# Block 0 of a state-space scan feeding a feed-forward product: the second scan moved into the second product, an idle product dropped, weight loads sent behind VectorE's steps

## The chip, the cores and the metric

The kernel runs on one core of a Trainium2 chip. Its time is device time in microseconds (us), given as the median of several runs of the whole program. One further execution was profiled: its trace says when each instruction of TensorE (PE, with its weight loads as PEld), VectorE (DVE), ScalarE (ACT), GpSimd (POOL) and the DMA queue of SyncE (SP) started, how long it took, and what ended the idle time before it. Each engine executes its own instructions strictly in the order in which the program holds them, and waits there for what the others must have done.

## The reference

The first half is a Mamba-2 scan over 4 batches, 8 heads, 768 tokens, with 32 values and 16 states per head, in chunks of tokens:

```python
cum = np.cumsum(log_a_chunk, axis=-1)
L = np.exp(cum[..., :, None] - cum[..., None, :]) * causal
M = einsum('bhin,bhjn->bhij', C, B) * L
y = einsum('bhij,bhjd->bhid', M, x) + einsum('bhin,bhnd->bhid', C, state) * np.exp(cum)[..., None]
state = np.exp(sum(log_a_chunk)) * state + sum_j(B_j x_j * np.exp(cum_end - cum_j))
```

The heads of one token are then laid side by side (256 values per token, 3072 tokens), and the second half is a feed-forward layer with 2048 inner columns:

```python
h = x @ w_in                                  # 256 -> 2048
g = h * np.clip(h + 3, 0, 6) / 6              # hardswish
out = g @ w_out                               # 2048 -> 256
```

The inputs of the scan are 32-bit floats. Both weight matrices arrive as 64-bit floats, and the kernel turns them into 32-bit ones itself.

## The kernel before

**Blocks.** The 768 tokens of a batch are cut into six blocks of 128. Block k holds these 128 tokens of all four batches, 512 rows of the feed-forward layer. Within a block the scan works in two halves of 64 tokens. While the feed-forward layer of block k runs, the scan of block k+1 is done between its products.

**Row sums.** The logarithms of `a` lie with one row per batch and head (32 rows, 768 columns, `a_sb`). VectorE's scan (`add_up`, L282) multiplies a running sum by `run` (one, and zero at each start of 64) and adds the logarithm. It is done in two parts: the first 256 columns (blocks 0 and 1), then the other 512 (blocks 2 to 5). The results of the second part go to DRAM by `store_rows` (L299, L301), and come back spread over partitions by `load_decay` (L314, the tile `L` of a block) and `load_eto` (L321, the tile `eto`); `rows(c)` calls both. They are also turned by TensorE (`turn_cum`, L329, into the bank `f1`) and copied with their sign changed by VectorE (`by_token`, L332, into `cum_n`). Blocks 0 and 1 get their exponents of decays from products of TensorE (`diff_*`), which ScalarE takes through the exponential (`diff_exp`, L393).

**A block's scan.** `scores(c)` (L558) makes the products of B and C, and L576 those of B and x for the new state. `multiply(c)` (L607) multiplies the four score banks with the decays on VectorE. `mix(c)` (L653) multiplies the result with x, and `from_state` (L531) adds what comes from the state; for that `csT` is C times the decay since the start (`fade`, L509). `keep(c)` (L667) copies the results on ScalarE into `yT`. `renew(c)` (L628, L586) makes the next state, which `carry` (L431) and `ends` (L424) on GpSimd use later. `conceal` (L158) masks a decay tile on GpSimd, `decay` (L413) exponentiates it on ScalarE.

**Weights.** `load_w(i)` (L139) loads an eighth of the weights, 1 MB, into one of three buffers `raw`: 0 to 3 are quarters of `w_in`, 4 to 7 of `w_out`. `decode(i)` turns it into 32-bit floats in steps, each up to a `yield`: a copy of the top halves on ScalarE (L198), masks on VectorE (L215, L217, L201, L205), two activations on ScalarE (L221, L223), and two last steps on VectorE (L228, L236). `weights(i, n)` does the next n steps.

**Feed-forward, block 0.** The first product (`mlp_in`, L677) makes 16 stripes f of 128 inner columns by 512 rows in plain 32-bit arithmetic, in the four banks f0 to f3 in turn; each stripe is two passes, for the two halves of the 256 inputs. ScalarE's ramp (L784) and VectorE's product with it (L789) make `gT`. The second product (`first_out`, L802) follows in four parts i (a quarter of `w_out` each) for four batches b. Between these calls stand the steps of the last weights and the scan of block 1. From block 1 on both factors of the first product are split into three parts (`in_parts`, L714 on ScalarE, L717 and L720 on VectorE, for the weights; `split_y`, L734, L735, L737, for the rows), and each stripe has three pairs of products (L745) in one of six banks: `squares` makes the first two pairs, `cross` the third after `enlarge` (L762 on VectorE for the first two stripes of block 1, L765 on ScalarE otherwise). So stripe f+6 of block 1 needs the bank of stripe f, which is free after its L789. The second product of these blocks works on sums of quarters (`weight_sums`, L828; `g_sums`, L848 on GpSimd; `wide_units`, L993).

**Order.** The order on each engine is that of the calls, written out by hand; only the waits are derived, from which instruction writes and reads which tile. Tiles with the same tag share a place. SyncE issues nearly all DMAs from one queue, in the order of the calls; a DMA at its head that has to wait for its buffer, or for data, holds all that stand behind it.

The tile `pre`, in which `a_sb`, `run` and the sums lie, shares its place with `gT` of block 0. `busy(n, bank)` (L521) runs n products of the identity with itself, whose results nobody reads.

```python
    multiply(0)
    load_w(3)
    c_ps = ps.tile([P, NC, G], FP32, name="c_ps", tag="f1")
    turn_cum(c_ps)
    busy(1, ps.tile([P, NB * P], FP32, name="d", tag="f0"))
    by_token(c_ps)
    weights(0, 1)
    weights(1, 1)
    mix(0)
    keep(0)
```

## Time and profile before

| | before |
|---|---|
| median of 3 runs | 337.82 us |
| the three runs | 338.59, 337.82, 337.63 us |
| the profiled execution's own time | 337.39 us |
| its span in the trace | 335.6 us |
| TensorE busy | 329.2 us (98%) |
| VectorE busy | 264.3 us (79%) |
| ScalarE busy | 208.0 us (62%) |
| GpSimd busy | 133.4 us (40%) |
| block 0's scores start (L558) | 15.07 us |
| block 0's own products start (L653) | 19.15 us |
| block 0's first product, start and length (L677) | 22.06 us, 27.74 us |
| block 0's second product starts (L802) | 49.80 us |
| block 1's first product starts (L745) | 82.68 us |

The times in the lower rows are counted from the start of the span. The span is a little shorter than the time of the execution, which also holds what lies before the first and after the last instruction. Busy time is a sum over the whole span, and says which engine could be the bound; which wait ends last in one place is read from the chain of work that ended last (each piece was released by the one before it) and from the instructions in order of time. In those, the number in brackets is the idle time of the engine before the instruction, with what ended it.

### The profile page before, as it was taken

How to read it: one execution, taken by the hardware profiler on the slowest of the kernel's cores; microseconds unless marked ns; L12 is line 12 of the kernel's file. 1: busy time of each engine (PE TensorE's matmuls, PEld its weight loads, DVE VectorE, ACT ScalarE, POOL GpSimd, SP SyncE). 2: the span in 40 equal slices, each digit the busy share in tenths (PEclk: the TensorE clock that was granted, in tenths of full speed). 3: DMA queues.
4: the chain of work that ended last, by engine and by line, in shares of the span. 5: the costliest groups of instructions: out<-in, count | busy, mean ns of one | idle time of the engine just before them, and what ended most of it. 6: DMA issues, size and time to landing. Idle time of an engine off the chain costs nothing.

```text
span 335.6 us, 8324 instructions
## 1 busy us (share of the span) xinstructions
PE 329.2 (98%) x3361; PEld 272.0 (81%) x3361; DVE 264.3 (79%) x416; ACT 208.0 (62%) x447; POOL 133.4 (40%) x125
## 2 busy tenths in 40 slices
PE   7999999999999999999999999999999999999995
PEld 5454788888888888888888888888888888899995
DVE  6999999998499739769949558938678958599974
ACT  4778878657986671677662477643487221677661
POOL 2400000290284799079983078771058740000000
PEclk9999999999999999999999999999999999999999
DMA  8998977042590216249107258100142001210001
GB/s 175 169 320 187 188 261 177 2 56 75 144 139 1 58 40 133 34 70 81 35 2 164 35 77 76 32 4 10 28 71 19 2 4 17 29 20 0 2 0 63
DMA packets 89605, 25.15 MB, mean 75 GB/s; under 512 B 82208, under 2 KB 85952, under 8 KB 89056
## 3 DMA queue, kind: packets, MB, share of 16 engines
q1 hardware_dynamic: 85184, 23.33, 37.4%
q10 hardware_dynamic: 4384, 1.31, 1.8%
q8 instruction: 26, 0.43, 0.5%
q14 instruction: 11, 0.09, 0.1%
HBM read 21.33 MB, written 3.29 MB: 73 GB/s over the span
## 4 chain that ended last, share of the span: by engine, by line
PE 96%; DVE 2%; issue 1%; POOL 0%; ACT 0%; POOLq 0%
PE h L745 33%; PE wc L993 8%; PE o L802 8%; PE wb L993 8%; PE h L677 8%; PE wa L993 8%; PE o_end L957 6%; PE wb L1001 3%; PE y L653 3%; PE y L531 2%; PE cb L558 2%; PE d L356 1%; DVE q_part L885 1%; PE d L521 1%; PE y L576 1%; PE d L369 1%
## 5 line engine op out<-in xcount | busy, mean ns | idle before, releaser
L789 DVE SCALAR_TENSOR_TENSOR gT<-gT,h 128x512 f32<-128x512 f32 x96 | 64.9, 684 | 24.9 <-ACT gT L784 23.3
L784 ACT ACTIVATE gT<-h,half 128x512 f32<-128x512 f32 x96 | 65.5, 684 | 23.4 <-PE h L745 21.3
L765 ACT ACTIVATE h<-h 128x512 f32<-128x512 f32 x66 | 38.3, 585 | 36.9 <-PE h L745 36.7
L745 PE MATMUL h<-y_hi,w_part 128*128 128x512 f32 x160 | 51.0, 404 | 0.0
L745 PE MATMUL h<-y_less,w_part 128*128 128x512 f32 x160 | 50.1, 400 | 0.0
L745 PE MATMUL h<-y_lo,w_part 128*128 128x512 f32 x160 | 49.5, 395 | 0.0
L848 POOL TENSOR_TENSOR s<-gT 128x512 f32<-128x512 f32 x16 | 24.9, 1559 | 48.0 <-DVE gT L789 48.0
L745 PEld LDWEIGHTS h<-y_lo,w_part 128*128 128x128 f32 x160 | 30.0, 188 | 6.9
L745 PEld LDWEIGHTS h<-y_hi,w_part 128*128 128x128 f32 x160 | 30.0, 188 | 6.8 <-DVE gT L789 0.2
L745 PEld LDWEIGHTS h<-y_less,w_part 128*128 128x128 f32 x160 | 29.1, 188 | 6.1 <-DVE h L762 0.3
L413 ACT ACTIVATE L<-L,cum_n 128x64 f32<-128x64 f32 x128 | 31.7, 337 | 0.0
L802 PE MATMUL o<-w_out,gT 128*128 128x256 f32 x128 | 28.8, 381 | 0.0
L677 PE MATMUL h<-yT,w_in 128*128 128x256 f32 (+1 forms) x94 | 27.8, 457 | 0.0
L802 PEld LDWEIGHTS o<-w_out,gT 128*128 128x128 f32 x128 | 24.1, 190 | 3.4
L677 PEld LDWEIGHTS h<-yT,w_in 128*128 128x128 f32 x94 | 17.8, 190 | 9.7 <-issue 6.9
L431 POOL TENSOR_TENSOR tmp<-state,eto 128x256 f32<-128x256 f32 x5 | 3.2, 632 | 56.2 <-ACT eto L417 48.7
L848 POOL TENSOR_TENSOR gT<-gT 128x512 f32<-128x512 f32 x16 | 23.9, 1501 | 0.7
L158 POOL TENSOR_SCALAR_AFFINE_SELECT L<-L 64x1024 f32<-64x1024 f32 (+1 forms) x16 | 20.6, 1297 | 8.2 <-DMA L<-cum_d 7.7
L885 DVE TENSOR_TENSOR q_part<-gT,q_part 128x256 fp32r<-128x256 f32 x24 | 21.6, 928 | 0.0
L424 POOL TENSOR_TENSOR bs<-B,L 128x128 f32<-128x128 f32 x24 | 12.7, 549 | 21.8 <-ACT L L413 14.1
L957 PE MATMUL o_end<-v_pair,g_pair 128*128 128x256 f32 x120 | 21.1, 281 | 0.0
L848 POOL TENSOR_TENSOR s<-s,gT 128x512 f32<-128x512 f32 x16 | 20.6, 1292 | 0.0
(164 smaller groups left out, 636.7 us busy)
## 6 DMA issues: line engine op xcount, KB each, us to landing
raw<-in_moe_w_out_dram SPq DMA_DIRECT2D x4, 1024.0 KB
L<-cum_d SPq DMA_DIRECT2D x8, 512.0 KB
xt<-in_x_dram SPq DMA_DIRECT2D x6, 512.0 KB
raw<-in_moe_w_in_dram SPq DMA_DIRECT2D x3, 1024.0 KB
out_dram<-back SPq DMA_DIRECT2D x128, 16.0 KB
pairs<-in_C_dram SPq DMA_DIRECT2D x40, 32.0 KB
eto<-cum_e SPq DMA_DIRECT2D x20, 64.0 KB
B<-in_B_dram SPq DMA_DIRECT2D x5, 256.0 KB
```

What stands on the lines that cost most here:

```text
L158: nc.gpsimd.affine_select(out=t[rows], in_=t[rows], pattern=pattern, compare_op=ALU.is_ge, fill=-1e5, base=base, channel_multiplier=-1)
L413: nc.scalar.activation(Ls[c][:, b, h], Ls[c][:, b, h], AF.Exp, bias=cum_n[:, c, g:g + 1])
L677: nc.tensor.matmul(out=h[:, t:t + n], lhsT=w_in[f // FP][:, j, f % FP * P:(f % FP + 1) * P], rhs=yTs[k][:, j].rearrange("p b i -> p (b i)" ...
L745: nc.tensor.matmul(out=hs_[k, f], lhsT=w[j][:, f % FP * P:(f % FP + 1) * P], rhs=y[:, j], start=(start and j == 0), stop=True, skip_group_ ...
L765: nc.scalar.activation(h, h, AF.Copy, scale=1.0 / EPS + 1.0)
L784: nc.scalar.activation(gTs[k][:, f], h, AF.Relu, bias=half, scale=1.0 / 6.0)
L789: nc.vector.scalar_tensor_tensor(out=g, in0=g, scalar=1.0, in1=h, op0=ALU.min, op1=ALU.mult)
L802: nc.tensor.matmul(out=o[:, b % 2], lhsT=gTs[0][:, f, b * P:(b + 1) * P], rhs=w_out[:, f], start=(f == 0 and b % 2 == 0), stop=True, skip_ ...
L848: nc.gpsimd.tensor_tensor(out=o, in0=p_, in1=q_, op=op)
L885: nc.vector.tensor_tensor(out=l[:, j], in0=g[:, j], in1=h[:, j].bitcast(FP32), op=ALU.subtract)
L957: nc.tensor.matmul(out=ends_["cross" if n == 2 else "squares"][b], lhsT=g_parts[t][n][:, b * P:(b + 1) * P], rhs=w, start=(t == 0 and b < ...
L993: nc.tensor.matmul(out=bank[:, slot], lhsT=lhs[:, j], rhs=rhs[:, j], start=(clear and j == 0), stop=True, skip_group_check=True)
```

## The change

Row sums: `a_sb`, `run` and the sums (`cum`) get places of their own, in the tags `t2`, `t3` and `y_lo`. The second scan, the storing of its sums, and the loads of block 1's `eto` move from the start behind block 0's first product (all stripes), ahead of the steps of the last two eighths of the weights. The renewal of the state moves from after block 0's copies to part (1, 0) of the second product; the four turns and `by_token` to part (1, 1), into the same bank. The idle product after the turns goes; the two ahead of the scores stay. The fade of block 0 is done by VectorE in place of GpSimd.

Weights: the decoding of the first eighth is taken a step further before the scores, with its last step split off by a new `yield`. The second eighth is loaded in two halves; the second half is sent by `load_rest`, after a memset of one of its columns by VectorE, which makes the DMA wait for VectorE's steps ahead of the memset. The third eighth is sent after such a memset too, behind `multiply(0)`. ScalarE's first copy of the second eighth is also done in halves, and the second one stands between block 0's copies.

Parts for block 1: the steps of `in_parts` for the first two quarters are called later within the second product, and those for the third quarter behind block 1's copies. The rows of block 3 are asked for before the end of the second product. Block 3's masks (`conceal`) are called at other stripes. One more product of block 0's first product is cut in two halves of 256 columns.

```diff
-    a_sb = pre[:G, 0:2].rearrange("g t i -> g (t i)")[:, :S]
+    rowed = [pool.tile([P, S], FP32, name="rowed", tag=tag, bufs=1)
+             for pool, tag in ((const, "t2"), (const, "t3"), (att, "y_lo"))]
+    a_sb, run, cum = (t[:G] for t in rowed)
...
+        raws[i] = raw
+        if i == 2:
+            nc.vector.memset(raw[:, :1], 0)
+        if i == 1:
+            queue.dma_start(out=dst[:, 0], in_=src[:, 0])
+            return lambda: (nc.vector.memset(dst[:, 1, :1], 0),
+                            queue.dma_start(out=dst[:, 1], in_=src[:, 1]))
         queue.dma_start(out=dst, in_=src)
-        raws[i] = raw
...
-    load_w(1)
+    load_rest = load_w(1)
...
-    run = pre[:G, 2:4].rearrange("g t i -> g (t i)")[:, :S]
...
-        nc.scalar.copy(out=s, in_=top)
+        for sl in (slice(0, n),) if i != 1 else (slice(0, n // 2), slice(n // 2, n)):
+            nc.scalar.copy(out=s[:, sl], in_=top[:, sl])
+            if i == 1 and sl.start == 0:
+                yield
...
         nc.vector.tensor_tensor(out=e, in0=e, in1=s, op=ALU.bitwise_or)
+        if i == 0:
+            yield
...
-    cum = pre[:G, 4:6].rearrange("g t i -> g (t i)")[:, :S]
...
-    def keep(c):
+    def keep(c, between=None):
...
+            if between and (a, u) == (0, 1):
+                between()
...
-            n = TB // (1 + (f * NK + j >= NF * NK - 15))
+            n = TB // (1 + (f * NK + j >= NF * NK - 16))
...
     diff(1, 0, 1)
-    weights(0, 1)
+    weights(0, 2)
     diff_exp(1, 2)
     diff_exp(1, 3)
     turn_squares(bcs[0][0], turned(0)[2])
     part_heads(0)
-    fade(0, HALF[1], nc.gpsimd)
-    add_up(ends_at[1])
-    store_rows()
-    load_w(2)
+    fade(0, HALF[1])
     weights(0, 1)
+    load_rest()
     busy(2, ps.tile([P, NB * P], FP32, name="d", tag="f3"))
     scores(0)
     multiply(0)
+    load_w(2)
     load_w(3)
-    c_ps = ps.tile([P, NC, G], FP32, name="c_ps", tag="f1")
-    turn_cum(c_ps)
-    busy(1, ps.tile([P, NB * P], FP32, name="d", tag="f0"))
-    by_token(c_ps)
     weights(0, 1)
     weights(1, 1)
     mix(0)
-    keep(0)
+    keep(0, lambda: weights(1, 1))
     weights(1, 3)
-    renew(0)
     weights(1, 1)
-    load_eto(1)
     load_bc(1)
...
+            weights(NP + 1, 1)
+            add_up(ends_at[1])
+            store_rows()
+            load_eto(c)
             rows(ahead)
-            weights(NP + 1, 1)
...
-            w_more = {(1, 1): (0, 0, 1), (2, 1): (1, 1, 2)}
+            w_more = {}
...
+                    if (i, b) == (1, 0):
+                        renew(0)
+                    if (i, b) == (1, 1):
+                        c_ps = ps.tile([P, NC, G], FP32, name="c_ps", tag="f1")
+                        turn_cum(c_ps)
+                        by_token(c_ps)
...
                         load_bc(ahead)
+                        for n in (0, 0, 1):
+                            next(ins[n])
...
-                        next(ins[2])
-                        next(ins[2])
+                        next(ins[1])
+                        next(ins[1])
...
                         results(c)
+                        next(ins[2])
                         decay(ahead, 2)
                     elif (i, b) == (3, 2):
+                        rows(ahead + 1)
...
             lead_on(c)
-            rows(ahead + 1)
+            next(ins[2])
+            next(ins[2])
...
-            if f in ((8, 12) if k == 1 else (3, 7)) and ahead < NC:
-                conceal(ahead, int(f in (7, 12)))
+            if f in ((3, 7)) and ahead < NC:
+                conceal(ahead, int(f == 7))
```

## The prediction

> **What bounds the kernel now.** I read the page first, then the chain that ended last, then the order in time of TensorE, VectorE and ScalarE from 12 to 110 us, which is all that the change touches.

> The page's busy times and its slices:

> ```profile
> PE 329.2 (98%) x3361; PEld 272.0 (81%) x3361; DVE 264.3 (79%) x416; ACT 208.0 (62%) x447; POOL 133.4 (40%) x125
> ...
> DVE  6999999998499739769949558938678958599974
> ...
> PEclk9999999999999999999999999999999999999999
> ```

> TensorE is busy 329.2 of 335.6 us, at full clock in every slice. So time is gained only by taking work or a wait from TensorE, and lost only where something new makes it wait. VectorE is nearly full in slices 2 to 9 (8 to 75 us) and again near 100 us: that is where TensorE's suppliers are tight.

> The chain, in order of time, columns start and length:

> ```profile
> 13.05 1.91 PE d L521 x4
> 14.97 0.11 issue
> 15.07 1.25 PE cb L558 x59
> 16.32 0.01 issue
> 16.33 1.30 DVE L L607 x2
> 17.62 0.04 issue
> 17.67 0.43 PE c_ps L329 x4
> 18.10 1.05 PE d L521 x2
> 19.15 0.90 PE y L653 x54
> ...
> 22.06 27.74 PE h L677 x94
> ```

> Between block 0's scores and its own products (L653) TensorE does two things that L653 does not need: the four turns of the row sums (L329, 0.43 us, for which it waits 0.61 us, since their bank is free only after the second L607) and an idle product (L521, 1.05 us).

> What stands ahead of block 0's copies on ScalarE, and the tight place near 100 us on VectorE and TensorE (start, length, engine, line):

> ```profile
> 18.53 1.15 ACT L198 COPY ws<-raw 128x1024 uint16<-128x1024 uint16 x1 [0.54 <-DMA raw<-in_moe_w_in_dram]
> 20.07 0.37 ACT L667 COPY yT<-y 128x256 f32<-128x256 f32 x1 [0.39 <-PE y L653]
> ```
> ```profile
> 92.47 0.69 DVE L789 SCALAR_TENSOR_TENSOR gT<-gT,h 128x512 f32<-128x512 f32 x1 [1.44 <-ACT gT L784]
> ...
> 98.95 2.23 DVE L828 TENSOR_TENSOR t<-w_out 128x1024 f32<-128x1024 f32 x1
> 101.10 1.27 DVE L789 SCALAR_TENSOR_TENSOR gT<-gT,h 128x512 f32<-128x512 f32 x2
> ```
> ```profile
> 101.88 0.68 PE L745 MATMUL h<-y_hi,w_part 128*128 128x512 f32 x2
> ```

> The second weights land at 18.53. At 101.88 TensorE starts stripe 14 of block 1 in the bank of stripe 8, whose L789 ends at 101.10+0.68 = 101.78: the slack there is 0.1 us, the smallest I find.

> **The head.** Scores still start at 15.07, because L503 ends at 14.93. On VectorE the scan (14.85 to 16.05) leaves; in its place come the fade (256 elements; L628, alike, takes 0.42), L228 (0.68) and a memset (L172, alike: 0.06), with pitches 0.45+0.72+0.06 from 14.85: 16.1, before the first L607 can start at 16.33. L228 needs ScalarE's L223, which moves ahead of the two L393 and ends at 14.8; those end at 15.8 and the products into the state (L576, 16.20) wait for them: covered by 0.4. So L607 stays at 16.33, 16.95, 17.57, 18.19, ending 18.81.

> L653's bank needs L592 (17.09 to 17.46), and its third product the second L607 (17.57): it starts at about 17.56 instead of 19.15. The rest is 0.90+0.61+0.79+0.61 = 2.91 from the chain; the second half needs the last L607 (18.81) only at 19.1. So L677 starts at 20.47 instead of 22.06: **1.59 us earlier**. The first weights are ready in time: VectorE loses L332 (0.28) and has L228 behind it, so L236 ends at 20.05.

> For this the copies must not come late. The second stripe pass needs both last copies by 20.47+0.86 = 21.33; two copies (0.64) and half an L198 (0.5) in front of them put the latest landing of the deferred half of the second weights at about 20.1. It is sent after the memset, 16.1. First bytes come 0.9 to 1.8 us after an issue (B sent at 68.83, bytes from 69.75; output weights sent at 46.4, a full stream from 48.2); 0.52 MB at the 0.40 MB/us seen from 48.5 to 50 take 1.3; the second weights' last bytes (about 17.9) were usable at 18.53, 0.6 later. That gives 18.9 to 19.8: in time, by 0.3 to 1.2.

> The third weights go behind L607, 18.9 instead of 16.94; by the same steps with 1.05 MB they land near 23.5, and ScalarE asks for them at 25.18-1.5 = 23.7. If 0.5 late, two L784 wait; their banks are wanted 2 us later. No cost.

> VectorE also loses renewal and row sums before L789 (0.42+0.61+pitch, 0.28): its first L789 moves from 26.61 to 25.1, as far as TensorE. L677 keeps its 27.74; one more product cut in halves is free by the same rows (32 stripe products of 0.867, whole or halved; bound 0 to 0.1).

> **The second product of block 0.** The four turns come here: **+0.43**, as the bank (stripe 13) and the scan (about 54.9) are done before 58.7. The scan's 1.20 delays the third and fourth output weights: third ready 61.07-1.5+1.2 = 60.8, wanted at 64.49-1.2 = 63.3; covered. Renewal, 1.3 with L332, follows the fourth, so csT ends near 65.8 (67.93 before), wanted at 70.2. On SP the row sums are stored at 54.9, read back from 57, about 61.5 for the first exponentials (wanted 63.7) and 66 for the masks (wanted 68.3); no output or load that is wanted sooner stands behind them. POOL loses the fade (1.51); its mask calls keep their order. These parts cost 0. So TensorE is 1.59-0.43 = 1.16 earlier at 81.

> **The first product of block 1.** Weight part 2 moves behind block 1's copies: on ScalarE two L714 (1.05) ahead of the 16 L413; on VectorE two pairs L717, L720 between the L762 (ending 85.05) and the first L789. The waits of VectorE there before were 1.53+0.47+0.70+1.44. ScalarE's L784 of stripe 3 then starts at 91.27 instead of 91.76: of the 1.16, only 0.49 is left, since ScalarE loses 1.05 and regains 0.3 of waits. VectorE's chain from that L789 to stripe 8's has no waits in it, and its end was TensorE's limit within 0.1. What is left there is therefore 0.5, changed by what POOL does beside it:

> ```profile
> L717 DVE SCALAR_TENSOR_TENSOR w_part<-w_part,w_in x8: 677/686/1625, 64.1 to 95.6; 128x512 fp32r<-128x512 f32 x8
> L720 DVE TENSOR_TENSOR w_part<-w_part x8: 691/739/1516, 64.8 to 96.3; 128x512 fp32r<-128x512 f32 x8
> ```

> (min/median/max ns.) The slow ones lie beside POOL's work. Block 3's rows are now asked for ahead of the second output, 80 instead of 87.2, so POOL's masks run about 86.7 to 92 instead of 92 to 98.8. The second pair (95.6, where L720 took 1.51) is freed: -0.8; the first gets a sum of POOL's (1.76) beside it: +0.5 to +0.8. I take -0.2: **0.7 us gained** at stripe 14 (bounds: nothing, if both pairs are slow; 1.16, if VectorE catches up). From there TensorE's order is unchanged and its chain is 96% its own, so the shift stays.

> [...]

> **Sum.** -1.59+0.43+0.46 = -0.7. The profiled execution is 337.39 (span 335.6 and 1.8 around it), giving 336.7; the median shown, 337.82, lies 0.43 above it, giving 337.1.

> **Rivals.**
> 1. *VectorE's moved pairs become the bound (slower).* Stripe 6 takes stripe 0's bank at 90.78-1.16 = 89.62, so stripe 0's L789 must start by 88.97, 3.9 us after the pairs may begin. They take 2.7 at their minima and 6.3 at their maxima. Above 3.9 TensorE waits, above 5.1 all the gain is gone; at 6.3 the result is 1.2 above before, 339.0. For it: masks run in this place. Against: only the last 1 us of the pairs overlaps them.
> 2. *The deferred half lands late.* Each us past 20.1 costs one; past 20.8 the gain is gone. The second weights' issue took 3.29 us on SP at 10.43, with small packets queued; such an issue instead of 0.4 means 22.0, and 1.2 slower: 339.0. Against: stores at 16.08 were issued in 0.34.
> 3. *No new wait near 100 us.* Then 1.16 and perhaps 0.1 of contention stay: 336.6.
> 4. *The clock falls without the idle product.* The wait of 0.61 at 17.06 passed at full clock; the new gap is 0.5. I give it nothing of its own.

> **How the numbers follow.** A change of 0.3% (1.0 us) is about what a measurement of this kernel can tell from none. Forecast (gain 0.3 to 1.16): 0.48, a quarter of it over 1.0. Rival 3: 0.22, faster. Rival 1: 0.17, of which 0.13 slower. Rival 2: 0.13, of which 0.10 slower. Faster 0.34, within 0.43, slower 0.23. The range is 336.3 to 338.7, which leaves out the upper ends of rivals 1 and 2 and the last tenths of rival 3; the forecast's own is 336.7 to 337.5.

> **What would show it.** L653 starts near 17.6 and L677 near 20.5, 0 to 0.3 us after the last copies. The half L198 on ScalarE starts before 20.1. L745 of stripe 14 is where the shift shrinks from 1.2 to 0.7. Wrong, if L677's second pass waits for ScalarE, if L653 is not before 18.5, or if the first L789 of block 1 starts after 89.

## The result, and the profile after

The changed kernel takes 341.91 us (median of 4 runs: 341.2, 342.8, 338.81, 342.63), the kernel before 337.73 in the same comparison. The ratio is 1.0106, 95% interval 1.0071 to 1.0142: about 1% slower, where 0.2% faster was forecast, and outside the forecast range. The profiled execution took 341.20 us, its span is 339.5. In the changed kernel all lines have higher numbers: L653 is now L664, L677 is L690, L531 is L542, L558 is L569, L667 is L680, L198 is L206, L576 is L587, L592 is L603, L789 is L802, L717 and L720 are L730 and L733, L745 is L758.

The page of the changed kernel, the lines that answer to those shown of before:

```profile
PE 331.4 (98%) x3361; PEld 272.9 (80%) x3361; DVE 266.7 (79%) x419; ACT 208.2 (61%) x448; POOL 130.6 (38%) x124
...
DVE  6877999978889729978958657957768958599973
...
PEclk9989999999999999999999999999999999999999
```

The new thing is the 8 in the third slice of the granted clock (17 to 25.5 us). There was none before. The chain of the changed kernel that ended last, for 15 to 30 us (start, length, what):

```profile
15.61 1.21 PE cb L569 x54
16.82 0.80 PE y L587 x53
17.62 0.02 issue
17.64 0.38 ACT adds L603
18.02 0.04 issue
18.07 0.94 PE y L664 x54
19.01 0.61 PE y L542 x16
19.62 0.26 PE y L664 x12
19.88 1.72 issue
21.60 0.75 PE y L664 x43
22.35 0.61 PE y L542 x16
22.96 7.04 PE h L690 x12
```

The turns and the idle product are gone, and L664 starts right behind the second score product. But in the middle of L664's second half TensorE stands for 1.72 us, and the releaser is "issue": nothing that the profile shows. The first stripe starts at 22.89 (first record) against 21.99 before, so the head is 0.90 later and not 1.59 earlier.

The windows of the changed kernel behind that (stretch, length; busy time and count of PE, PEld, DVE, ACT, POOL; then granted clock, DMA share, GB/s):

```profile
20.00:23.50 3.50, 1.90 (x70) 1.49 (x70) 2.61 (x5) 1.55 (x5) 0.00 (x0) 1.00 0.86 277
23.50:27.00 3.50, 3.50 (x6) 1.44 (x5) 1.91 (x3) 2.94 (x4) 0.00 (x0) 0.51 1.01 387
27.00:30.50 3.50, 3.50 (x9) 1.55 (x9) 2.61 (x6) 1.99 (x3) 0.00 (x0) 1.00 1.24 295
```

From 23.52 to 26.93 us, for 3.413 us, TensorE gets half its clock, though it is busy all the time (6 products start in that stretch, 9 in the next). That costs half of 3.4, about 1.7 us (an estimate from the length of the stretch).

Where the time went, by the starts of TensorE's stages in the two traces:

| stage | before | after | difference |
|---|---|---|---|
| first stripe of block 0 starts | 21.99 | 22.89 | +0.90 |
| block 0's first product | 27.65 | 29.35 | +1.70 |
| block 0's second product, to block 1's first | 33.04 | 33.70 | +0.66 |
| block 1's first product | 22.50 | 22.98 | +0.48 |
| from there to TensorE's last product | 226.53 | 226.48 | -0.05 |

The sum is 3.69; another 0.15 lies behind TensorE's last product. The span grew by 3.83, the time by 3.81. (Block 1's first product is counted from where the one ahead of it ends, 82.68 in the kernel before; its first record is at 82.33, and counted from there the stage takes 22.86 and 23.33.) So the two things that the forecast did not have at all, the wait and the half clock, are the result; the other two stages lost about what it said, 1.14 instead of 0.89.

### The profile page after: what moved, and what is told of

Its sections match the earlier page's. It is cut to its first block, busy times and chain, and to the rows that moved or that the text cites. A ratio compares the mean times of both kernels' runs of the same rounds, so it can differ in the third digit from the quotient of the medians.

```text
span 339.5 us, 8329 instructions
## 1 busy us (share of the span) xinstructions
PE 331.4 (98%) x3361; PEld 272.9 (80%) x3361; DVE 266.7 (79%) x419; ACT 208.2 (61%) x448; POOL 130.6 (38%) x124
## 3 DMA queue, kind: packets, MB, share of 16 engines
q1 hardware_dynamic: 85200, 23.33, 36.2%
HBM read 21.33 MB, written 3.29 MB: 73 GB/s over the span
## 4 chain that ended last, share of the span: by engine, by line
PE 96%; DVE 1%; issue 1%; POOL 0%; ACT 0%; POOLq 0%
PE h L758 33%; PE h L690 9%; PE wc L1006 8%; PE o L815 8%; PE wb L1006 8%; PE wa L1006 8%; PE o_end L970 6%; PE wb L1014 3%; PE y L664 3%; PE y L542 2%; PE cb L569 2%; PE d L367 1%; PE y L587 1%; DVE q_part L898 1%; PE d L380 1%
## 5 line engine op out<-in xcount | busy, mean ns | idle before, releaser
L802 DVE SCALAR_TENSOR_TENSOR gT<-gT,h 128x512 f32<-128x512 f32 x96 | 64.8, 684 | 22.7 <-ACT gT L797 21.2
L797 ACT ACTIVATE gT<-h,half 128x512 f32<-128x512 f32 x96 | 65.6, 685 | 25.1 <-PE h L758 21.1
L758 PE MATMUL h<-y_hi,w_part 128*128 128x512 f32 x160 | 51.2, 405 | 0.0
L758 PE MATMUL h<-y_less,w_part 128*128 128x512 f32 x160 | 50.1, 399 | 0.0
L758 PE MATMUL h<-y_lo,w_part 128*128 128x512 f32 x160 | 49.5, 395 | 0.0
L758 PEld LDWEIGHTS h<-y_hi,w_part 128*128 128x128 f32 x160 | 29.9, 188 | 7.3 <-DVE gT L802 0.8
L758 PEld LDWEIGHTS h<-y_lo,w_part 128*128 128x128 f32 x160 | 30.0, 188 | 6.9
L758 PEld LDWEIGHTS h<-y_less,w_part 128*128 128x128 f32 x160 | 29.1, 188 | 6.2 <-DVE h L775 0.3
L690 PE MATMUL h<-yT,w_in 128*128 128x256 f32 (+1 forms) x96 | 29.5, 471 | 0.0
L690 PEld LDWEIGHTS h<-yT,w_in 128*128 128x128 f32 x96 | 18.7, 196 | 10.4 <-issue 7.8
L166 POOL TENSOR_SCALAR_AFFINE_SELECT L<-L 64x1024 f32<-64x1024 f32 (+1 forms) x16 | 20.5, 1284 | 1.6 <-DMA L<-cum_d 1.1
L435 POOL TENSOR_TENSOR bs<-B,L 128x128 f32<-128x128 f32 x24 | 11.8, 521 | 23.1 <-ACT L L424 15.7
L861 POOL TENSOR_TENSOR s<-s,gT 128x512 f32<-128x512 f32 x16 | 20.6, 1297 | 0.0
```

The lines of the kernel that those rows point to most:

```text
L166: nc.gpsimd.affine_select(out=t[rows], in_=t[rows], pattern=pattern, compare_op=ALU.is_ge, fill=-1e5, base=base, channel_multiplier=-1)
L690: nc.tensor.matmul(out=h[:, t:t + n], lhsT=w_in[f // FP][:, j, f % FP * P:(f % FP + 1) * P], rhs=yTs[k][:, j].rearrange("p b i -> p (b i)" ...
L758: nc.tensor.matmul(out=hs_[k, f], lhsT=w[j][:, f % FP * P:(f % FP + 1) * P], rhs=y[:, j], start=(start and j == 0), stop=True, skip_group_ ...
L797: nc.scalar.activation(gTs[k][:, f], h, AF.Relu, bias=half, scale=1.0 / 6.0)
L802: nc.vector.scalar_tensor_tensor(out=g, in0=g, scalar=1.0, in1=h, op0=ALU.min, op1=ALU.mult)
L861: nc.gpsimd.tensor_tensor(out=o, in0=p_, in1=q_, op=op)
```

## The experiments

**The theories.** *Code*: the wait is for TensorE's own program. The instruction queue moved 26 packets of 16 KB in both kernels:

```profile
q8 instruction: 26, 0.43, 0.5%
```

TensorE has 3361 products and as many weight loads, with its semaphore instructions 6753 records in the kernel before. By these counts a packet holds 6753/26, about 260 of them, at 16384/260, about 63 bytes each, an estimate. One such packet ends 1.27 us before TensorE goes on at 21.60; the DMA view of the changed kernel from 19.3 to 20.4 us:

```profile
DMA packets 18, 0.06 MB, mean 52 GB/s; under 512 B 7, under 2 KB 7, under 8 KB 17
...
q8 instruction: 1, 0.02, 5.3%
```

Counted in order of start, from 0 and with its semaphore instructions, the first instruction behind the wait is the 705th of TensorE's records. (This order is not quite the program's, and "strictly in the order" above is too strong for TensorE: right ahead of this wait come five weight loads in a row, at 19.59 to 19.61 us, and then six products, at 19.63 to 19.66; the last of these loads belongs to the product at 21.60, behind all six.) Boundaries at 193 + 256 k fit the whole trace: there are 26 of them among the 6753 records of the kernel before (6754 after) and 26 packets, and taken in order each packet starts between 3.5 us ahead of its boundary's record and 4.0 us behind it. So the packets of this queue are those of TensorE's program.

*Data*: the wait is for something that the products read, and the profile names it wrongly. *Traffic* (later *queue*): the weight transfers that the change moved stand in the way of what TensorE waits for. *Clock*: the idle product held the clock up.

**E1: 40 instructions fewer ahead.**

```diff
-            for _ in range(30):
+            for _ in range(10):
```

> The changed kernel with 10 instead of 30 of the 1x1 products of the mask's setup, so TensorE's program has 40 instructions fewer (20 products, 20 weight loads) ahead of block 0's scores; no wait or transfer changes. The new wait of TensorE stood in the middle of block 0's own products, after the 12th product of their second half (19.88 to 21.60 us). Theory 'code': the wait is for TensorE's own program, which arrives 256 instructions at a time, and stands at instruction 768 of it. Then it moves by 20 products: past the 12th, to about the 32nd product of the second half, and is shorter, about 1.2 to 1.4 us, since it starts some 0.3 us later and ends when it did, or 0.3 later still. Theory 'data': the wait is for something that these products read (the decayed scores, x, a bank) and the profile names it wrongly. Then it stays at the 12th product, to within a product or two, and keeps 1.5 to 1.9 us.

TensorE in order of time, with idle time before in brackets:

```profile
15.26 1.20 PE L569 MATMUL cb<-cT,bT 32*64 32x128 f32 x64 [0.47 <-DVE cT L514]
16.38 0.72 PE L587 MATMUL y<-xt,bs 64*32 64x64 f32 x49
19.06 0.34 PE L587 MATMUL y<-xt,bs 64*32 64x64 f32 x15 [1.96 <-issue]
19.93 1.12 PE L664 MATMUL y<-L,xt 64*32 64x64 f32 x64 [0.52 <-ACT adds L603]
20.98 1.11 PE L542 MATMUL y<-csT,mid 32*64 32x64 f32 x16
22.02 0.68 PE L664 MATMUL y<-L,xt 64*32 64x64 f32 x32
23.98 0.68 PE L664 MATMUL y<-L,xt 64*32 64x64 f32 x32 [1.28 <-issue]
```

The wait moved by exactly 20 products, from behind the 12th of the second half to behind the 32nd, though these read the same tiles. A second wait appeared 127 products ahead of it (15+64+16+32), at the 449th record: one packet earlier. That falls to "code" and against "data". (That the wait stands at instruction 768 was the author's estimate; by the records it is the 705th.) The second one was not forecast. The one run took 344.43 us, with three steps of half clock (10.24 us).

**E2: the idle product put back, ahead of the products with x.**

```diff
+    busy(1, ps.tile([P, NB * P], FP32, name="d", tag="f0"))
     mix(0)
```

> The changed kernel with one idle product (1.05 us) put back, ahead of block 0's own products. By the sum on record this costs the whole 1.05, at 342.0 to 343.0 against 341.9 for the changed kernel. Theory 'code': the time was TensorE's to lose: the wait inside block 0's own products shrinks from 1.7 to 0.6-1.0 us, the first stripe of block 0 starts at 22.9 to 23.2 as without the idle product. Theory 'clock': a gap of 1.0 us or less there leaves the granted clock at full speed from 22 to 28 us; without the half clock of 3.4 us the run is 1.7 us shorter than the changed kernel's profiled 341.2: 339.5, and stays at 338.5 to 340 over the rounds. If the half clock has nothing to do with that gap, it is seen here too, and the time is 341 to 343.

Measured: 340.30 us (339.37 to 342.66, 5 runs), ratio 1.0065 (1.0041 to 1.0088). The wait did not shrink: in the profiled run, the slowest, it was 2.27 us, 19.81 to 22.08, again at the 705th record; and the clock was halved for 6.8 us. So an idle product does not by itself keep the clock up, and both theories missed here: "code" because the packet itself came later (it started at 19.73, against 19.40). The three runs with no half clock lie at 339.4 to 340.3. By the sum of the prediction this kernel should take 1.05 more than the changed one; the intervals of the two ratios overlap, with this one the lower. E8, E9 and E10 below have none in the head; E8 and E9 kept full clock there and E10 did not.

**E3: more instructions ahead, where TensorE waits anyway.**

```diff
-    busy(2, ps.tile([P, NB * P], FP32, name="d", tag="f3"))
+    idle = ps.tile([P, NB * P], FP32, name="d", tag="f3")
+    for _ in range(78):
+        nc.tensor.matmul(
+            out=idle[:1, :1], lhsT=ident_h[:, :1], rhs=hide[:, :1], start=True, stop=True,
+            skip_group_check=True)
+    busy(1, idle)
```

> The changed kernel with the two idle products ahead of the scores replaced by 78 products of 1x1 and one idle product: 156 instructions of TensorE more, at a place where it waits anyway (the scores start when VectorE is done). Nothing else changes. Theory 'code': the count of 256 is crossed earlier, the next block of the program is asked for earlier and is there when TensorE comes to it. Then no wait of 1.7 us inside block 0's own products, the first stripe of block 0 starts at 20.5 to 21.2 (22.96 in the changed kernel, 22.06 before), the clock stays full, and the time is 336.5 to 338.0, against 341.9 and 337.7. Theory 'data' (something the products read is late): the wait keeps 1.5 to 1.9 us and its product, and the time stays 341 to 343.

TensorE in order of time:

```profile
18.41 0.47 PE L664 MATMUL y<-L,xt 64*32 64x64 f32 x16 [0.46 <-ACT adds L603]
20.00 0.72 PE L664 MATMUL y<-L,xt 64*32 64x64 f32 x48 [1.12 <-issue]
20.65 0.68 PE L542 MATMUL y<-csT,mid 32*64 32x64 f32 x16
21.26 0.86 PE L664 MATMUL y<-L,xt 64*32 64x64 f32 x64
25.65 0.58 PE L542 MATMUL y<-csT,mid 32*64 32x64 f32 x7 [3.54 <-issue]
```

The place was right and the hope wrong. 76 products more moved the wait from product 92 of this stage (64+16+12) to product 16, and 128 products further on stands the next one, of 3.54 us: two packet boundaries now lie among the small products. Four more waits, of 0.7 to 2.1 us, stand at later boundaries (82 to 237 us). The two quicker runs took 349.98 and 352.13 us, ratio 1.0394 (1.0349 to 1.0439); the other two, with a granted clock of 0.974, took 355.30 and 356.61.

**E4: the weight loads of before.** Both halves at the start, the third weights ahead of the scores.

```diff
-    load_rest = load_w(1)
+    load_w(1)()
...
-    load_rest()
+    load_w(2)
```

> The changed kernel with the weight loads of before: both halves of the second weights sent at the start, the third weights at the place of the deferred half, no transfer sent behind VectorE's fade or behind the decayed scores. Theory 'traffic': the changed kernel's transfers (0.5 MB at 16.3 us, 1 MB at 19.4) stood in front of what TensorE waited for at 19.88. Then the wait of 1.7 us is gone or under 0.8, and the first stripe of block 0 starts by 22.0. Theory 'code': TensorE's program is asked for when TensorE gets there, whatever the weights do, and the wait stays 1.2 to 1.9 us at the same product, with the half clock behind it; 340.5 to 342.5.

342.09 us (one run). The wait was 1.42 us, at the same product, and the clock was halved for 6.8 us. So the deferral is not what makes the wait.

**E5: the kernel before without its idle product.**

```diff
-    busy(1, ps.tile([P, NB * P], FP32, name="d", tag="f0"))
```

> The kernel before with its idle product ahead of block 0's own products taken out, and nothing else. By the sum on record that idle product lies on the path: 1.05 us less, 336.6 to 336.9. Theory 'code': TensorE then comes to the boundary of its program (the 705th recorded instruction, 20.63 us before) at about 19.6, where the block was usable at 19.9 in the profiled execution before and at 20.7 to 22.0 in the others. So a wait of 0.3 to 1.9 us stands after about the 10th product of the second half of block 0's own products, the first stripe starts 0.7 us earlier at best and 0.9 later at worst, and the time is 337.0 to 338.6, with a half clock of 3.4 us in some runs.

TensorE in order of time:

```profile
17.85 0.43 PE L329 MATMUL c_ps<-ident,pre 32*128 32x32 f32 x4 [0.61 <-DVE L L607]
18.21 0.86 PE L653 MATMUL y<-L,xt 64*32 64x64 f32 x64
19.00 0.68 PE L531 MATMUL y<-csT,mid 32*64 32x64 f32 x16
19.61 0.32 PE L653 MATMUL y<-L,xt 64*32 64x64 f32 x8
20.14 0.78 PE L653 MATMUL y<-L,xt 64*32 64x64 f32 x56 [0.22 <-issue]
20.85 0.68 PE L531 MATMUL y<-csT,mid 32*64 32x64 f32 x16
21.46 4.99 PE L677 MATMUL h<-yT,w_in 128*128 128x512 f32 x11
```

This is the wait in its smallest form: behind the 8th product, four places ahead of the changed kernel's 12th, because the four turns still stand ahead. The idle product was 1.05 us long; the first stripe came 0.53 earlier, in an execution whose scores started 0.1 later. The median was 337.27 against 338.11; but two of the ten runs (340.35 and 341.10) had a granted clock of 0.99 instead of 1.00, and with them the ratio is 0.9998 (0.9970 to 1.0026): not to be told from no change.

**E10, E8, E9: move the boundary.** 50 products of 1x1 in place of the two idle ones ahead of the scores; in E10 on E5, in E8 on the changed kernel, in E9 on the changed kernel with the splitting of weight part 2 back in its old places.

```diff
-    busy(2, ps.tile([P, NB * P], FP32, name="d", tag="f3"))
+    idle = ps.tile([P, NB * P], FP32, name="d", tag="f3")
+    for _ in range(50):
+        nc.tensor.matmul(
+            out=idle[:1, :1], lhsT=ident_h[:, :1], rhs=hide[:, :1], start=True, stop=True,
+            skip_group_check=True)
```

and in E9, and again in E12:

```diff
-            w_more = {}
+            w_more = {(1, 1): (0, 0, 1), (2, 1): (1, 1, 2)}
...
-                        for n in (0, 0, 1):
-                            next(ins[n])
...
                         renew(c)
-                        next(ins[1])
-                        next(ins[1])
+                        next(ins[2])
+                        next(ins[2])
...
                         results(c)
-                        next(ins[2])
...
             lead_on(c)
-            next(ins[2])
-            next(ins[2])
```

> The kernel before, without its idle product, and with the two idle products ahead of the scores replaced by 50 products of 1x1 (about 1.3 us, where TensorE waits until 15.1). That puts 100 - 8 - 4 = 88 instructions more ahead of the same place, so the boundary that stood at 705 falls 44 products earlier, in the first half of block 0's own products, its request ahead of the wait for the scores' inputs, and the next boundary behind the small products. Theory 'code': no wait without a releaser, the 1.05 us is gained in full: first stripe at 20.9 to 21.2 instead of 22.06, 336.4 to 337.0. If an idle product holds the clock, the half clock appears and the time is 338 to 340.

> The changed kernel with the two idle products ahead of the scores replaced by 50 products of 1x1: 92 instructions more ahead of the same place. Theory 'code': the boundary of the 705th instruction falls at about the 46th product of the first half of block 0's own products, asked for before the scores and there when TensorE comes (18.2); the next boundary falls some 10 products into the first stripes, asked for at about 17.6 and wanted at 23 or later. So no wait of over 0.3 us without a releaser, first stripe at 20.4 to 21.0, full clock throughout, and 336.3 to 337.6: the head's 1.6 us gained, less the four turns (0.43) and the 0.48 that the first product of block 1 lost. Theory 'the idle products hold the clock': half clock in 20 to 30 us without a gap, 339 to 342.

> As the run before it (50 small products for the two idle ones), and with the first product's splitting of weight part 2 back at the places it had in the kernel before (weight part 2 behind step (2,1), two more behind the renewal), everything else of the change kept. Expected by the trace of the changed kernel: the first product of block 1 takes 22.85 us as before instead of 23.33, so 0.3 to 0.5 us less than the run before it: 335.9 to 337.2. If the 0.48 came from elsewhere (POOL's sum and masks, which stay moved), the two runs are within 0.15 us of each other.

All three were far slower: E10 350.76 (ratio 1.0371, 1.0315 to 1.0428), E8 351.66 (1.0399, 1.0384 to 1.0414), E9 353.88 us (1.0475, 1.0450 to 1.0501). In block 0 the boundary fell where it should, behind the 46th product in E8 (43rd in E10), with a wait of 0.81 (1.36 in E10) that was not expected. The rest is later. TensorE's waits in E8 (total, times, longest) and one of them in order of time:

```profile
PE y L542 <- issue: 6.5, 4, 2.0
...
PE y L664 <- issue: 0.8, 1, 0.8
```

```profile
125.49 0.68 PE L542 MATMUL y<-csT,mid 32*64 32x64 f32 x29
127.59 0.33 PE L542 MATMUL y<-csT,mid 32*64 32x64 f32 x3 [1.42 <-issue]
```

The shift moved every later boundary too, and boundaries that had cost nothing now show as waits at the small products (L542) of blocks 2 to 5. Their records are the 3009th, 4033rd, 5057th and 6081st: 9, 13, 17 and 21 times 256 behind the 705th. Of the 26 waits of over 0.2 us that the profile puts down to "issue" between 15 us and TensorE's last product, in E1, E3, E5, E8, E9 and E10, 25 stand at 705 plus or minus a multiple of 256. The other, 0.41 us in E9 at 16.79, does not; it ends right behind ScalarE's L404 (16.70). Two half clocks of 3.4 us follow in E8, at 182 and 233 us.

**E11, E12, E13: when the deferred half is sent.** E11 sends it ahead of the fade (14.90 us instead of 16.34), E13 behind the decayed scores (18.80); E12 is E11 with the splitting of weight part 2 as before.

```diff
+    load_rest()
     fade(0, HALF[1])
     weights(0, 1)
-    load_rest()
```

and in E13:

```diff
     weights(0, 1)
-    load_rest()
...
     multiply(0)
+    load_rest()
```

> The changed kernel with the deferred half of the second weights (and the memset before it) sent ahead of VectorE's fade and the last step on the first weights instead of behind them: issued at about 15.1 instead of 16.3. The block of TensorE's program that starts at the 705th recorded instruction is asked for when the block before it is entered (449th, at 16.3 to 17.0); its packet started 0.8 to 1.4 us later in the runs with no weights sent in the half microsecond before that, and 2.0 to 3.5 later in those with. Theory 'queue' (the packet stands behind the weights sent just before it): packet 0.8 to 1.5 us behind the 449th, wait at the 705th 0 to 0.8 us, first stripe at 20.6 to 22.0, full clock in most runs, 337.5 to 338.8. If what the weights do has no part in it: packet 2.4 or more behind, wait 1.4 or more, half clock, 340.5 to 343.

> The changed kernel with the deferred half sent behind the four products of the decayed scores, with the third weights, at about 19: nothing is sent between 14 and 19 us. Theory 'queue': the packet of TensorE's program starts 0.7 to 1.2 us behind the 449th instruction, which is 17.7 to 18.2, and the wait at the 705th is 0 to 0.6 us. The deferred half lands at 22 or later, so ScalarE's last two copies wait for it and the first stripe stalls at its second pass: 339 to 342 in all, of which no part is said to be the program's. If the packet is late all the same (2 us or more behind the 449th), the weights are not its cause.

> The changed kernel with the half sent sooner as in the run before it, and with the splitting of weight part 2 back at the places of the kernel before. Block 1's first product took 22.50 us in the kernel before, 22.94 to 23.18 in five runs with the changed places, 22.49 in one run with the old ones. By that 0.5 us less than the run before it: 337.0 to 338.3, and 22.4 to 22.6 for block 1's first product. If the places of weight part 2 are not what costs there: 22.9 to 23.2 again, and no difference between the two.

TensorE in E13:

```profile
17.46 0.94 PE L664 MATMUL y<-L,xt 64*32 64x64 f32 x64 [0.46 <-ACT adds L603]
18.33 0.68 PE L542 MATMUL y<-csT,mid 32*64 32x64 f32 x16
18.94 0.33 PE L664 MATMUL y<-L,xt 64*32 64x64 f32 x12
19.57 0.75 PE L664 MATMUL y<-L,xt 64*32 64x64 f32 x52 [0.30 <-issue]
20.25 0.68 PE L542 MATMUL y<-csT,mid 32*64 32x64 f32 x16
20.86 1.13 PE L690 MATMUL h<-yT,w_in 128*128 128x512 f32 x2
```

With nothing sent between 14 and 18.8 us the packet started 1.03 us behind the 449th record, the wait was 0.30, and the first stripe started at 20.86. In E11 it was 1.50 and the wait 1.03, in E12, which sends the half at 15.03, 1.81 and 1.12; in the changed kernel 2.44 and 1.72. That is the order that "queue" asks for, from one profile each. E11 took 338.67 us (338.28 to 341.91, 10 runs), ratio 1.0052 (1.0030 to 1.0075): three quarters of the loss in the median against the changed kernel are gone, and half of it by the ratio, above all because six of ten runs had no half clock. E13 then paid for the late half (341.88, one run): ScalarE's half L206 started at 23.23, TensorE waited 2.48 us for the copy behind it, and a step of half clock followed.

E12 took 338.66 us, ratio 1.0027 (1.0014 to 1.0041). Its block 1 product took 22.47 us against 23.04 in E11, and E9's 22.49 against 23.18 in E8: the places of weight part 2 cost 0.6 to 0.7 there. But the medians of E11 and E12 hardly differ, so this gain is shown in the stage and not in the whole.

**E14: the kernel before, without the idle product, third weights later.**

```diff
+        if i == 2:
+            nc.vector.memset(raw[:, :1], 0)
...
-    load_w(2)
...
     multiply(0)
+    load_w(2)
...
-    busy(1, ps.tile([P, NB * P], FP32, name="d", tag="f0"))
```

> The kernel before without its idle product, and with the third weights sent behind the four products of the decayed scores (about 19 us) instead of at 16.9, behind a memset of 0.06 us on VectorE. Theory 'queue and code': in the kernel before without its idle product TensorE's block was asked for at 16.59 and its packet started 1.36 us later, with the third weights sent 0.3 us behind the request; the wait that was left at the 705th instruction was 0.22 us, and 2 of 10 runs were disturbed by a half clock. With nothing sent there the packet starts 0.8 to 1.1 us behind the request, the wait is 0 to 0.1, the first stripe starts at 21.2 to 21.4 instead of 22.06, and the time is 336.7 to 337.2 against 337.6 to 338.1 for the kernel before, with fewer half clocks. If the third weights now land too late (over 25 us), ScalarE's next tanh waits and the time is 337.5 or more.

336.85 us (336.43 to 337.45, 11 runs) against 337.78: ratio 0.9972 (0.9963 to 0.9981), faster than both kernels, and none of the 11 runs had a clock under 0.998. The reason given for it is not what the trace shows: the packet started 1.58 us after the block before it was entered, not 0.8 to 1.1, and the wait was 0.49, in a profiled execution that was the slowest of the runs (337.45), with the first stripe at 21.69. So the time came out as forecast and the reason did not. In this execution no step of the clock had over 0.96 us of idle time; why none of the other ten runs was hit is open.

The packets of all profiled executions, from the records of the instruction queue (us; the block before is entered at the 449th record, TensorE wants the block at the 705th):

| kernel | block before entered | packet starts | packet ends | TensorE there | goes on | wait |
|---|---|---|---|---|---|---|
| before | 16.40 | 17.66 | 18.62 | 20.63 | 20.63 | none |
| after | 16.96 | 19.40 | 20.33 | 19.88 | 21.60 | 1.72 |
| E1 | 19.06 | 21.80 | 22.75 | 22.70 | 23.98 | 1.28 |
| E2 | 16.26 | 19.73 | 20.68 | 19.81 | 22.08 | 2.27 |
| E3 | 16.16 | 16.95 | 18.61 | 18.88 | 20.00 | 1.12 |
| E4 | 16.46 | 18.45 | 19.42 | 19.39 | 20.80 | 1.42 |
| E5 | 16.59 | 17.95 | 18.92 | 19.93 | 20.14 | 0.22 |
| E8 | 15.94 | 16.73 | 17.86 | 18.50 | 19.31 | 0.81 |
| E9 | 15.81 | 17.48 | 18.41 | 18.81 | 19.71 | 0.90 |
| E10 | 15.99 | 18.06 | 19.02 | 18.95 | 20.31 | 1.36 |
| E11 | 16.75 | 18.25 | 19.22 | 19.67 | 20.70 | 1.03 |
| E12 | 16.45 | 18.26 | 19.23 | 19.38 | 20.50 | 1.12 |
| E13 | 16.35 | 17.38 | 18.32 | 19.27 | 19.57 | 0.30 |
| E14 | 16.54 | 18.12 | 19.07 | 19.88 | 20.37 | 0.49 |

In every row with a wait TensorE goes on 1.2 to 1.5 us after its packet has ended. The packet starts 0.8 to 3.5 us after the block before it was entered. That it waits in a queue behind the weights fits E11, E13 and the changed kernel; it does not fit all rows. E3 sent the half at 16.10, 0.06 ahead of the entry, and E8 at 16.30, 0.43 ahead of its packet, and both had 0.79; E14 sent no weights between 14 and 18.98 and had 1.58. By these the two groups named ahead of E11 do not hold, and the cause of the delay is not settled. No record shows when a block is asked for: that this is when the one before it is entered was the author's assumption (E8, E10, E11, E14).

## Why the prediction was wrong

**The head** is the step that failed, at "So L677 starts at 20.47 instead of 22.06: 1.59 us earlier". What the step says of data on the way to the first stripe held, but for the landing of the deferred half (below): where the scores started as early as before, L664 started at 17.46 to 17.58 (E13, E4, E12), against 17.56 forecast, and with a wait of only 0.30 the first stripe came at 20.86. In the profiled execution of the changed kernel L664 is 0.5 later, since full clock began at 9.86 us after the span's start instead of 8.24 and the work ahead of the scores ran longer (products of 512 columns start 0.427 us apart ahead of that, L375 at 6.43, and 0.217 behind it, L380 at 10.98). Of the 2.49 us between the head forecast and the head measured, 1.72 are the wait, 0.51 are this, and 0.26 is that the small products behind L664's start took 3.17 without the wait, and not 2.91. What the step left out is that TensorE must have its program. In the kernel before the block from the 705th record on was there at about 18.62 + 1.3 = 19.9, worked out with the delay of the other rows; TensorE came at 20.63. So of the 1.59 us only 0.7 were to be had, even with the packet as early as before (E13, whose packet ended 0.3 earlier, gained 1.13 at the first stripe). The idle product and the wait for the turns looked like work on the path; 0.7 us of them could go, and the rest hid the packet's delay. The signs were on the page: an instruction queue of 0.43 MB against TensorE's count, and a stretch of 288 small products (64 scores, 64 for the state, 160 of its own) that passes 128 products, those of the scores and of the state, in 2 us (15.07 to 17.06).

**Rival 4, "The clock falls without the idle product. ... I give it nothing of its own."** This is the other half of the loss, by another way than named. It isn't the missing idle product (E2 has it and lost the clock, E8 and E9 lack all of them and kept it there), but the idle time that the wait brings. The clock's records change at steps of 3.413 us: up to TensorE's last product the stretches at one clock are 13.653, 3.413 and 314.026 us long in the changed kernel and 327.679 in the one before, which is 4, 1, 92 and 96 steps. In the changed kernel TensorE was idle for 1.50 us of the step from 20.10 to 23.52, and the next step ran at half clock. In the fourteen traces, from 8 us to TensorE's last product, a step at full clock with 1.6 us of idle time or more was followed by half clock all eleven times (E4's 1.60 and E13's 2.48 among them), and one with less than 1.39 never was (0.62 before, 1.03 in E11, 1.36 in E9). Between these both happened: 1.40 (E12) and 1.48 (E2) lost the clock, 1.51 (E10) and 1.59 (E3) kept it, so there is no clean threshold. Why the half clock lasted for two or three steps in some executions is open. The steps lie differently in each execution (one begins at 8.24 us in the kernel before, at 9.86 in the changed one), so the same wait is split differently: the four runs of the changed kernel had clocks of 0.995, 0.990, 0.998 and 0.990, and by 1.7 us for each 0.005 they would be at about 339.5, 339.4, 338.8 and 339.2 without it, an estimate. Single gaps of 1.1 to 1.7 us (1.12 in E12, 1.42 in E4, 1.72 in the changed kernel), 1.40 to 1.60 us of idle time in one step, were enough.

**Rival 2, the deferred half.** Forecast at 18.9 to 19.8, needed by 20.1. ScalarE in the changed kernel, in order of time:

```profile
20.66 0.64 ACT L206 COPY ws<-raw 128x512 uint16<-128x512 uint16 x1 [0.62 <-DMA raw<-in_moe_w_in_dram]
22.37 0.37 ACT L680 COPY yT<-y 128x256 f32<-128x256 f32 x1 [1.07 <-PE y L664]
```

It was usable at 20.66, 4.3 us after its issue at 16.34, where 2.8 to 3.7 were forecast, so 0.6 past the limit. It cost nothing because the copy behind it waited for TensorE until 22.37. With L664 0.5 later, as here, the same sum puts the limit at 20.6, so without the wait for the program the half would have come right at it; no run shows that case.

**The second product of block 0.** Forecast +0.43 for the turns; 33.04 grew to 33.65 to 33.74 in the changed kernel, E1, E2, E4, E8, E11 and E13, +0.6 to +0.7. The turns are all that is new on TensorE there. In the changed kernel 0.56 of its 0.66 stand at the turns and the products around them, and 0.1 at block 1's own small products.

**The first product of block 1.** Forecast a loss of 0.46, measured 0.48 (22.50 to 22.98), and by the cause named, weight part 2 on VectorE, but not in the place named. VectorE in the changed kernel, in order of time:

```profile
89.42 0.68 DVE L730 SCALAR_TENSOR_TENSOR w_part<-w_part,w_in 128x512 fp32r<-128x512 f32 x1
90.14 0.83 DVE L733 TENSOR_TENSOR w_part<-w_part 128x512 fp32r<-128x512 f32 x1
90.89 1.11 DVE L730 SCALAR_TENSOR_TENSOR w_part<-w_part,w_in 128x512 fp32r<-128x512 f32 x1
92.04 1.51 DVE L733 TENSOR_TENSOR w_part<-w_part 128x512 fp32r<-128x512 f32 x1
93.47 1.87 DVE L802 SCALAR_TENSOR_TENSOR gT<-gT,h 128x512 f32<-128x512 f32 x3
...
97.67 1.66 DVE L733 TENSOR_TENSOR w_part<-w_part 128x512 fp32r<-128x512 f32 x1
99.25 1.27 DVE L802 SCALAR_TENSOR_TENSOR gT<-gT,h 128x512 f32<-128x512 f32 x2
```

The two pairs took 4.05 us, between the minima (2.7) and maxima (6.3) of the first rival and just over its 3.9; the second pair has 2.62 of it, beside GpSimd's masks. TensorE falls back by 0.26 at stripe 6, which needs the bank of the first L802: that is the first rival's place. It falls back by 0.23 more at stripe 10, behind the L802 that follows the slow L733 at 97.67, and by nothing at stripe 14. The 0.46 was worked out as the part of an early arrival that gets lost at stripe 14, and block 1 arrived late here; E9 and E12 show that the places cost 0.6 to 0.7 by themselves. E5, which arrived 0.6 earlier with the old places, did lose 0.3 at stripe 14; but E10, which arrived 3.8 later with the old places, lost 0.4 at stripe 12, so these losses are not all from an early arrival. The size was right by luck. No run shows the 0.1 of contention that the third rival adds: with GpSimd's work moved and the old places the stage took 22.49 in E9 and 22.47 in E12, against 22.50 before.

## What to carry to other kernels

Before taking a wait or an idle product out of a stretch of many small products, count TensorE's instructions and mark every 256th. (In the traces here the boundaries lay at 193 + 256 k of the recorded ones, so the first has to be found from a wait.) From the entry into one block to the use of the next this chip needed 3.2 to 5.8 us here (the table's "goes on" less "entered", in the rows with a wait), so a stretch that passes 128 products faster than that can wait for its program, as it did in thirteen of the table's fourteen kernels; and adding instructions in one place moves all boundaries behind it, which cost more here (13 to 16 us) than the change that it was to mend. A wait that the profile puts down to "issue" should be counted in instructions before it is explained; and waits that add up to 1.4 us or more in one step of 3.413 us cost another 1.7 us or more by the clock, in some executions and not in others.
